# Spreading the attention normalisers by two transfers, and pairing batches so that 64-token blocks fill a matmul

## The chip, the cores and the metric

The kernel runs on one core of one Trainium2 chip. Times are device microseconds (us). Runs are compared within one call on one chip, beside runs of the kernel before; each is marked fast or slow by its clock and time, and only fast runs are compared.

## The reference

```python
scores = (q @ k.T) / sqrt(64) + cum[:, None] - cum[None, :]   # 8 batches, 8 heads, 576 tokens, causal
attn   = exp(scores - max);  attn /= attn.sum(-1)
x      = attn @ v                                             # heads side by side: 8 x 576 x 512
xk, xr = mu_k * x + (1 - mu_k) * x_prev, mu_r * x + (1 - mu_r) * x_prev
out    = sigmoid(xr @ w_r) * (relu(xk @ w_k) ** 2 @ w_v)
```

The first half is attention with a forget gate, the second a channel mix whose inputs blend each token with the one before.

## The kernel before

The attention works on pairs of heads and keeps its output transposed, 128 partitions (two heads of 64) by 576 tokens. So dividing by the softmax sum needs, on all 64 partitions of a head, the same row of 576 reciprocals. TensorE collects the sums in `den`, VectorE transposes, takes reciprocals and transposes back into `R`, and this row is spread through DRAM, for two pairs of heads (a group) at a time:

```python
PARTS = [(0, 384), (384, 192)]        # the 576 tokens in two parts ("halves")

def norm(g):
    dT = dT_ring()
    nc.vector.transpose(dT, den[:, 0:32 * QB])              # QB = 12: 384 columns
    nc.vector.reciprocal(rt[:, :, 0:2], dT[:, :, 0:2])
    nc.vector.transpose(R, rt)                              # row 32*(2*half+hh)+j is used

def spread_norm(g):
    scr = scr_ring()                                        # DRAM, [4, 32, 384]
    nc.sync.dma_start(out=scr, in_=R)
    rb = rb_ring()                                          # SBUF, [128, 2, 576]
    for half, (q0, n) in enumerate(PARTS):
        for hh in range(2):
            nc.sync.dma_start(
                out=rb[hh * D:(hh + 1) * D, :, q0:q0 + n],
                in_=scr[2 * half + hh, 0:2, 0:n].unsqueeze(0).to_broadcast([D, 2, n]))
```

Then `values` multiplies: `x = nm * rb`, once per half. The first two of sixteen groups take another way (`spread_now`, a matmul), so there are 14 such spreads. The channel mix goes in blocks of 128 tokens. A batch is 4.5 blocks, so every odd batch begins with a block that straddles two batches; it was made of two matmuls of 64 output rows each, placed side by side in the array (line L472), where other blocks take one (L468). The order of all work is written out by hand in strings of slots (`FIRST`, `ROUND`, `DRAIN`), each letter one operation.

The softmax here doesn't subtract the row's maximum and nothing guards it: scores larger than these inputs give would overflow.

Of the kernel before, what the change touches and what calls it, by code (L numbers as in the profile page):

```python
# [9 lines left out]
F32 = mybir.dt.float32  # L10
BF16 = mybir.dt.bfloat16
AF = mybir.ActivationFunctionType
ALU = mybir.AluOpType
# [19 lines left out]
PARTS = [(0, 384), (384, 192)]  # L33
QB = PARTS[0][1] // 32
# [3 lines left out]
def kernel(  # L38
# [13 lines left out]
    nc = tc.nc  # L52
    B, H, S, D = q.shape
    Dm = H * D
    Dff = moe_w_k.shape[1]
    P = 128
    SCALE = 1.0 / (D ** 0.5)
    BH = B * H
    NC = 5
    NP = BH // 2  # L60
    n_db, n_fb = Dm // P, Dff // P
    HB = S // 2
# [24 lines left out]
    mm_ring = Ring(3, [P, 512], F32, "mm", mmp)  # L87
    scr_ring = Ring(2, [4, 32, 32 * QB], F32, "scr", drp)
    a_ring = Ring(4, [P, 2, AW], BF16, "a")
    rb_ring = Ring(3, [P, 2, S], F32, "rb")  # L90
    qb_ring = Ring(2, [P, 4, P], BF16, "qb")
    kb_ring = Ring(2, [P, 4, P], BF16, "kb")
    xk_ring = Ring(2, [P, n_db, S], BF16, "xk")
    xr_ring = Ring(3, [P, n_db, S], BF16, "xr")
    sq_ring = Ring(2, [P, n_fb, S], BF16, "relusq")
    dT_ring = Ring(2, [P, QB, 32], F32, "dT")
    diff_ring = Ring(2, [P, S], BF16, "diff")
    rel_ring = Ring(3, [P, 2, HB], BF16, "rel")
# [39 lines left out]
                                   in_=(q, k, v)[i][b, hs, 4 * P:, :].rearrange("h p d -> p h d"))  # L138

    chain = [rb_ring() for _ in range(2)]  # L140
    lf, cum, wrow, zrow = (chain[i // 2][:BH, i % 2, :] for i in range(4))
    nc.scalar.dma_start(out=lf, in_=f_bh[:, :])
    load(q, qf[0], 0)
    load(k, kf[0], 0)
# [7 lines left out]
    mu_k_sb = cp.tile([P, n_db], F32)  # L152
    nc.sync.dma_start(out=mu_k_sb, in_=moe_mu_k.rearrange("(db p) -> p db", p=P))
    mu_r_sb = cp.tile([P, n_db], F32)
# [19 lines left out]
    R = cp.tile([P, QB, 32], F32)  # L174
# [5 lines left out]
    for j in range(2):  # L180
        for half in range(2):
            for hh in range(2):
                v_ = sel[:, j, half, hh * D:(hh + 1) * D]
                nc.gpsimd.affine_select(
                    out=v_, in_=v_, compare_op=ALU.not_equal, fill=1.0,
# [123 lines left out]
    def load_weights(i):  # L309
        dst, src = ((wk_sb, moe_w_k), (wr_sb, moe_w_r), (wv_sb, moe_w_v))[i]  # L310
        nc.gpsimd.dma_start(out=dst, in_=src.rearrange("(n p) d -> p n d", p=P))
# [3 lines left out]
    rbs = {}  # L315
# [31 lines left out]
    for kb in range(NC):  # L347
        for part, (p0, pn) in enumerate(PARTS):
            q0 = max(kb * P, p0)
# [29 lines left out]
    def spread_norm(g):  # L379
        scr = scr_ring()  # L380
        nc.sync.dma_start(out=scr.rearrange("g r c -> (g r) c"),
                          in_=R.rearrange("p a b -> p (a b)"))
        rb = rb_ring()
        for half, (q0, n) in enumerate(PARTS):
            for hh in range(2):
                nc.sync.dma_start(  # L386
                    out=rb[hh * D:(hh + 1) * D, :, q0:q0 + n],
                    in_=scr[2 * half + hh, 0:2, 0:n].unsqueeze(0).to_broadcast([D, 2, n]))
        for i in range(2):
            rbs[2 * g + i] = rb[:, i, :]  # L390

    def spread_now(Pi, copy):

        g, j = divmod(Pi, 2)
        if j == 0:
            rb = rb_ring()
            for i in range(2):
                rbs[2 * g + i] = rb[:, i, :]
        for half, (q0, n) in enumerate(PARTS):
            rp = mm_ring()  # L400
            nc.tensor.matmul(rp[:, 0:n], lhsT=sel[:, j, half, :],
                             rhs=R.rearrange("p a b -> p (a b)")[:, 0:n], start=True, stop=True)
            copy(rbs[Pi][:, q0:q0 + n], rp[:, 0:n])

    def values(Pi, half):
        a = aw[Pi]
        nm = mm_ring()
        b, p = divmod(Pi, PRW)
        t, tl = vw[Pi % NV], vt[b % 2]
        for kb, hf, col, o, n, last in PIECES:  # L410
            if hf != half:
                continue
            for r0 in range(0, P, 32):
                hh, d0 = divmod(r0, D)
                w = t[:, kb, hh] if kb < 4 else tl[:, 2 * p + hh]
                nc.tensor.matmul(  # L416
                    nm[r0:r0 + 32, o:o + n],
                    lhsT=w[:, d0:d0 + 32],
                    rhs=a[:, hh, col:col + n],
                    start=(kb == 0), stop=last,  # L420
                    tile_position=(0, r0))
        q0, n = PARTS[half]
        nc.vector.tensor_tensor(out=xs[Pi % NX][:, 1 + q0:1 + q0 + n], in0=nm[:, 0:n],  # L423
                                in1=rbs[Pi][:, q0:q0 + n], op=ALU.mult)
        if half == 1:
            aw.pop(Pi)
            rbs.pop(Pi)

    xks = {}
    xrs = {}  # L430

    def shift(Pi):
        b, p = divmod(Pi, PRW)
        if p == 0:
            xks[b] = xk_ring()
            xrs[b] = xr_ring()
        x = xs[Pi % NX]
        diff = diff_ring()
        nc.vector.tensor_sub(diff, x[:, 1:S + 1], x[:, 0:S])
        for dst, mu in ((xks[b], mu_k_sb), (xrs[b], mu_r_sb)):  # L440
            nc.vector.scalar_tensor_tensor(out=dst[:, p, :], in0=diff, scalar=mu[:, p:p + 1],  # L441
                                           in1=x[:, 0:S], op0=ALU.mult, op1=ALU.add)


    rsq = {}
    rels = {}

    def key_unit(b, hf, fb):
        if hf == 0 and fb == 0:
            rsq[b] = sq_ring()  # L450
        kp = mm_ring()
        for db in range(n_db):
            nc.tensor.matmul(kp[:, :HB], lhsT=wk_sb[:, db, fb * P:(fb + 1) * P],  # L453
                             rhs=xks[b][:, db, hf * HB:(hf + 1) * HB],
                             start=(db == 0), stop=(db == n_db - 1))
        if fb % 2 == 0:
            rels[b, hf] = rel_ring()
        rel = rels[b, hf]
        nc.scalar.activation(rel[:, fb % 2, :], kp[:, :HB], func=AF.Relu)  # L459
        if fb % 2 == 1:  # L460
            nc.vector.tensor_mul(rsq[b][:, fb - 1:fb + 1, hf * HB:(hf + 1) * HB], rel, rel)  # L461



    def block_mms(ps, tiles, b, t0, w, n):
        for i in range(n):
            if t0 >= 0:
                nc.tensor.matmul(ps, lhsT=tiles[b][:, i, t0:t0 + P], rhs=w[:, i, :],  # L468
                                 start=(i == 0), stop=(i == n - 1))
            else:  # L470
                for lo, t in ((0, tiles[b - 1][:, i, S - 64:S]), (64, tiles[b][:, i, 0:64])):
                    nc.tensor.matmul(ps[lo:lo + 64, :], lhsT=t, rhs=w[:, i, :],  # L472
                                     start=(i == 0), stop=(i == n - 1),
                                     tile_position=(0, lo))

    gates = {}

    def gate_unit(b, t0):
        rp = mm_ring()
        block_mms(rp, xrs, b, t0, wr_sb, n_db)  # L480
        th = th_ring()
        nc.scalar.activation(th, rp, func=AF.Tanh, scale=0.5)  # L482
        gates[b, t0] = th
# [21 lines left out]
    def queue_mix(b):  # L505
        blocks = ((0, 128), (256, 384)) if b % 2 == 0 else ((-64, 64), (192, 320, 448))
        for hf in range(2):
            for fb in range(n_fb):
                keys.append((b, hf, fb))
            for t0 in blocks[hf]:  # L510
                gvs.append((b, hf, t0, gate_unit))
                gvs.append((b, hf, t0, value_unit))

    def run_keys(n):
        for _ in range(min(n, len(keys))):
            key_unit(*keys.popleft())
# [12 lines left out]
    def finish_mix(b):  # L529
# [15 lines left out]

    FAST = 4
    FIRST = (
        "S0 C f M T F M L3 L4 M S1 k",
        "M L M c W0 S0 M S1 T D",
        "M T W2 D N k L S0 b0 S1 M M",  # L550
        "M A0 S0 c M D M L W1 b1 T S1",
        "S0 H0 D N t M A1 S1 M L c M",
        "B2 H1 T S0 W3 M A2 H2 c B3 A3 S1 M M H3 D L",
        "Z Q0 S0 L D S1 W N K1 T M k P M M",
        "M K3 S0 K3 L t K2 A D H S1 c M M G W V",
        "S0 L T D c W A N S1 H M M P M",
        "G c K2 S0 K2 M T M W V S1 D V M G A H L",
        "S0 M K2 M T L K1 D S1 N P A W M c H G",
    )
    ROUND = (  # L560
        "S0 V T L R M K2 D c A G N V S1 M K2 P G H M W",
        "S0 L V K1 W M M T k K3 S1 M D V A H R",
        "S0 W G T c L M K3 G G S1 M A D N K1 G R P M H",
        "S0 V M T G W L K2 c D S1 M A R M H K2",
    )
    DRAIN = "K5 D N G P A W H G K3 R"
    WEIGHTS = (2, 3, 5)
    av_slot = {Pi: Pi + LAG for Pi in range(FAST, NP)}
    av_slot[NP - 1] -= 1
    mix_slot = {av_slot[b * PRW + PRW - 1] + 1: b for b in range(1, B)}  # L570
# [10 lines left out]
    def step(s, op, x):  # L581
# [31 lines left out]
        elif op == "P" and s <= NP:  # L613
            spread_norm(s // 2 - 1)
        elif op in "Bb":
            spread_now(x, nc.scalar.copy if op == "B" else nc.vector.tensor_copy)
        elif op == "W":
            for Pi in [x] if x is not None else [Pi for Pi in av_slot if av_slot[Pi] == s + 1]:
                weigh(Pi)
        elif op == "A":  # L620
            for Pi in avs:
                values(Pi, 0)
                values(Pi, 1)
# [28 lines left out]
    for s in range(NP + LAG):  # L652
        if s in WEIGHTS:
            load_weights(WEIGHTS.index(s))
        if s in mix_slot:
            queue_mix(mix_slot[s])
        for op in (FIRST[s] if s < len(FIRST) else ROUND[s % PRW] if s < NP else DRAIN).split():
            step(s, op[0], int(op[1:]) if op[1:] else None)
# [36 lines left out]
```

## Time and profile before

| | before |
|---|---|
| median at the time of prediction | 295.09 us (293.64 to 297.48) |
| TensorE busy, span of the profiled run (299.94 us, marked slow) | 266.5 of 298.2 us |
| mean granted clock of TensorE | 0.977 |
| VectorE idle for the spread | 12.0 us in 12 waits |

The only profile of the kernel before is of a run marked slow, some 2% above its fastest; where a difference is as small as that, this profile does not decide it.

From the page's slices (40 equal parts of the span, clock granted to TensorE and mean share of the 16 DMA engines busy, in tenths) and its list of DMA issues (transfer, count, size, median us to landing), kernel before:

```profile
PEclk9999799978999999999988999999999999999999
DMA  7999996854759494939584594949471915131112
...
rb<-scr SPq DMA_DIRECT2D x28, 192.0 KB, 3.3
...
rb<-scr SPq DMA_DIRECT2D x28, 96.0 KB, 3.3
```

The clock is nearly full throughout. Spreads of 192 and of 96 KB land alike, 3.3 us after issue.

### The profile page before, as it was taken

How to read it: one execution, taken by the hardware profiler on the slowest of the kernel's cores; microseconds unless marked ns; L12 is line 12 of the kernel's file. 1: busy time of each engine (PE TensorE's matmuls, PEld its weight loads, DVE VectorE, ACT ScalarE, POOL GpSimd, SP SyncE). 2: the span in 40 equal slices, each digit the busy share in tenths (PEclk: the TensorE clock that was granted, in tenths of full speed). 3: DMA queues.
4: the chain of work that ended last, by engine and by line, in shares of the span. 5: the costliest groups of instructions: out<-in, count | busy, mean ns of one | idle time of the engine just before them, and what ended most of it. 6: DMA issues, size and time to landing. Idle time of an engine off the chain costs nothing.

```text
span 298.2 us, 8098 instructions
## 1 busy us (share of the span) xinstructions
PE 266.5 (89%) x3194; PEld 159.0 (53%) x3221; DVE 226.1 (76%) x462; ACT 204.6 (69%) x360; POOL 88.0 (30%) x117
## 2 busy tenths in 40 slices
PE   1677878769899999999969999999989999999994
PEld 0344545335555655566535655566555656655551
DVE  6758989787978988789847977797968886874431
ACT  4878688457877878588865887688777875424530
POOL 7294227262333333223322424132322111000000
PEclk9999799978999999999988999999999999999999
DMA  7999996854759494939584594949471915131112
GB/s 211 237 258 202 242 230 190 206 142 146 208 150 262 126 300 121 282 112 270 151 240 135 150 274 119 278 114 290 115 223 65 250 35 185 65 115 70 68 41 106
DMA packets 82438, 52.06 MB, mean 175 GB/s; under 512 B 50336, under 2 KB 77216, under 8 KB 82400
## 3 DMA queue, kind: packets, MB, share of 16 engines
q1 hardware_dynamic: 80080, 48.75, 57.5%
q0 software_dynamic: 2096, 2.62, 5.1%
q8 instruction: 25, 0.41, 0.6%
q10 hardware_dynamic: 224, 0.18, 0.3%
q14 instruction: 13, 0.11, 0.1%
HBM read 41.96 MB, written 12.19 MB: 182 GB/s over the span
## 4 chain that ended last, share of the span: by engine, by line
PE 65%; DVE 11%; DMA 9%; ACT 9%; issue 2%; SPq 2%; DVEq 0%; ACTq 0%
PE mm L468 25%; PE mm L453 15%; PE mm L416 7%; PE sc L328 7%; DMA rb<-scr 6%; ACT a L334 5%; PE sc L233 4%; PE den L364 3%; PE mm L472 3%; ACT qkT L244 2%; DMA scr<-R 2%; SPq L386 2%; DVE x L423 2%; DVE a L340 2%; ACT rel L459 1%
## 5 line engine op out<-in xcount | busy, mean ns | idle before, releaser
L334 ACT ACTIVATE a<-sc 128x1024 bf16<-128x1024 f32 (+1 forms) x128 | 100.3, 842 | 17.0 <-PE sc L328 16.8
L453 PE MATMUL mm<-xk,wk_sb 128*128 128x288 bf16 x512 | 73.9, 289 | 1.5 <-DVE x L423 0.7
L468 PE MATMUL mm<-wv_sb,relusq 128*128 128x512 bf16 x246 | 61.4, 387 | 3.3 <-DVE x L423 2.7
L459 ACT ACTIVATE rel<-mm 128x288 bf16<-128x288 f32 x128 | 48.4, 417 | 16.4 <-PE mm L453 13.0
L453 PEld LDWEIGHTS <-wk_sb 128*128 128x128 bf16 x512 | 48.0, 99 | 21.0 <-issue 6.3
L220 POOL TENSOR_TENSOR vw<-vf,wbf 128x512 bf16<-128x512 f32 x32 | 34.5, 1077 | 72.8 <-DMA vf<-in_v_dram 30.1
L461 DVE TENSOR_TENSOR relusq<-rel 128x576 bf16<-128x576 bf16 x64 | 34.2, 544 | 28.0 <-ACT rel L459 27.9
L340 DVE TENSOR_TENSOR a<-a,bound 128x256 bf16<-128x256 bf16 (+2 forms) x96 | 44.7, 477 | 3.6 <-ACT a L334 3.3
L482 ACT ACTIVATE th<-mm 128x512 f32<-128x512 f32 x36 | 21.5, 598 | 34.7 <-PE mm L468 28.7
L328 PE MATMUL sc<-qkT 64*128 64x64 bf16 (+4 forms) x384 | 37.3, 291 | 8.2 <-ACT a L334 3.8
L468 PEld LDWEIGHTS <-relusq 128*128 128x128 bf16 x256 | 23.6, 99 | 32.2 <-issue 8.1
L244 ACT COPY qkT<-sc 128x1024 bf16<-128x1024 bf16 x29 | 29.4, 1014 | 14.8 <-PE sc L237 14.3
L423 DVE TENSOR_TENSOR x<-mm,rb 128x384 bf16<-128x384 f32 x64 | 27.1, 454 | 14.7 <-DMA rb<-scr 12.0
L209 POOL CAST qb<-qf 128x512 bf16<-128x512 f32 x22 | 18.1, 825 | 62.6 <-PE sc L233 37.4
L468 PE MATMUL mm<-wr_sb,xr 128*128 128x512 bf16 x111 | 32.6, 387 | 1.6 <-issue 0.3
L489 DVE SCALAR_TENSOR_TENSOR res<-th,mm 128x512 f32<-128x512 f32 x36 | 24.6, 683 | 12.4 <-PE mm L468 8.1
L328 PEld LDWEIGHTS <-qkT 64*128 64x128 bf16 x384 | 15.0, 96 | 30.3 <-issue 24.1
L416 PE MATMUL mm<-a,vw 128*32 128x192 bf16 (+3 forms) x896 | 29.5, 267 | 0.7 <-ACT rel L459 0.4
L441 DVE SCALAR_TENSOR_TENSOR xk<-diff,mu_k_sb,x 128x576 bf16<-128x576 bf16 x32 | 26.4, 826 | 1.1
L441 DVE SCALAR_TENSOR_TENSOR xr<-diff,mu_r_sb,x 128x576 bf16<-128x576 bf16 x32 | 26.0, 812 | 0.0
L416 PEld LDWEIGHTS <-vw 128*32 128x32 bf16 x896 | 20.4, 99 | 6.8 <-issue 4.4
L233 PE MATMUL sc<-ident,qb 128*128 128x128 bf16 x128 | 13.2, 230 | 8.4 <-DVE qb L209 5.3
(67 smaller groups left out, 237.0 us busy)
## 6 DMA issues: line engine op xcount, KB each, us to landing
out_dram<-res SPq DMA_DIRECT2D x36, 256.0 KB, 3.5
qf<-in_q_dram SPq DMA_DIRECT2D x32, 256.0 KB, 4.3
kf<-in_k_dram SPq DMA_DIRECT2D x32, 256.0 KB, 4.5
vf<-in_v_dram SPq DMA_DIRECT2D x64, 128.0 KB, 4.2
rb<-scr SPq DMA_DIRECT2D x28, 192.0 KB, 3.3
scr<-R SPq DMA_DIRECT2D x14, 192.0 KB, 1.9
rb<-scr SPq DMA_DIRECT2D x28, 96.0 KB, 3.3
vt_f<-in_v_dram SPq DMA_DIRECT2D x8, 128.0 KB, 5.4
```

The lines of the kernel that those rows point to most:

```text
L220: nc.gpsimd.tensor_tensor(out=vw[Pi % NV], in0=vf[Pi % NV], in1=wbf[:, :4, 2 * Pi:2 * Pi + 2].unsqueeze(3).to_broadcast([P, 4, 2, D]), op= ...
L244: copy(qkT[Pi % NQK][:, lo * S:hi * S].rearrange("p (i s) -> p i s", i=n)[:, :, 0:4 * P] .rearrange("p i (j c) -> p i j c", c=4), tp[:, 4 ...
L328: nc.tensor.matmul(sc[:, hh, w:w + n], lhsT=t[lo:lo + D, S + kb * P:S + (kb + 1) * P], rhs=t[lo:lo + D, q0:q0 + n], start=True, stop=True)
L334: nc.scalar.activation(out=a[:, :, off:off + w], in_=sc[:, :, 0:w], func=AF.Exp, scale=SCALE)
L340: nc.vector.tensor_tensor(out=v_, in0=v_, in1=bound[:, o:o + w].unsqueeze(1).unsqueeze(1).to_broadcast([P, 2, n, w]), op=ALU.min)
L416: nc.tensor.matmul(nm[r0:r0 + 32, o:o + n], lhsT=w[:, d0:d0 + 32], rhs=a[:, hh, col:col + n], start=(kb == 0), stop=last, tile_position=(0 ...
L423: nc.vector.tensor_tensor(out=xs[Pi % NX][:, 1 + q0:1 + q0 + n], in0=nm[:, 0:n], in1=rbs[Pi][:, q0:q0 + n], op=ALU.mult)
L441: nc.vector.scalar_tensor_tensor(out=dst[:, p, :], in0=diff, scalar=mu[:, p:p + 1], in1=x[:, 0:S], op0=ALU.mult, op1=ALU.add)
L453: nc.tensor.matmul(kp[:, :HB], lhsT=wk_sb[:, db, fb * P:(fb + 1) * P], rhs=xks[b][:, db, hf * HB:(hf + 1) * HB], start=(db == 0), stop=(db ...
L459: nc.scalar.activation(rel[:, fb % 2, :], kp[:, :HB], func=AF.Relu)
L461: nc.vector.tensor_mul(rsq[b][:, fb - 1:fb + 1, hf * HB:(hf + 1) * HB], rel, rel)
L468: nc.tensor.matmul(ps, lhsT=tiles[b][:, i, t0:t0 + P], rhs=w[:, i, :], start=(i == 0), stop=(i == n - 1))
```

## The change

The intent: spread a group's normalisers by two transfers instead of four, to save two issues of 0.6 us; lay two batches side by side in `xr` and the squared keys, so that the straddling block is contiguous and takes full matmuls; and retune the slots. Core of the diff:

```diff
-        for half, (q0, n) in enumerate(PARTS):
-            for hh in range(2):
-                nc.sync.dma_start(
-                    out=rb[hh * D:(hh + 1) * D, :, q0:q0 + n],
-                    in_=scr[2 * half + hh, 0:2, 0:n].unsqueeze(0).to_broadcast([D, 2, n]))
+        for half in range(2):
+            nc.sync.dma_start(
+                out=rb[:, half].rearrange("p j c -> p (j c)"),
+                in_=scr[2 * half:2 * half + 2, 0:2, :].rearrange("g j c -> g (j c)")
+                .unsqueeze(1).to_broadcast([2, D, 2 * 32 * QB]))
...
-    xr_ring = Ring(3, [P, n_db, S], BF16, "xr")
-    sq_ring = Ring(2, [P, n_fb, S], BF16, "relusq")
+    xr_ring = Ring(2, [P, n_db, 2, S], BF16, "xr")
+    sq_ring = Ring(2, [P, n_fb, 2, S], BF16, "relusq")
...
+        t0 += b % 2 * S
         for i in range(n):
-            if t0 >= 0: ...one matmul...  else: ...two of 64 rows, side by side...
+            nc.tensor.matmul(
+                ps, lhsT=tiles[b // 2][:, i].rearrange("p b s -> p (b s)")[:, t0:t0 + P],
+                rhs=w[:, i, :], start=(i == 0), stop=(i == n - 1))
...
-        "S0 V T L R M K2 D c A G N V S1 M K2 P G H M W",      (ROUND, first of four; all slots changed)
+        "S0 V L R t M K2 V D A N S1 K2 c P G H M M W",
-    WEIGHTS = (2, 3, 5)
+    WEIGHTS = (0, 3, 5)
```

## The prediction

> **What bounds the kernel now.** I read first the busy shares of the engines, then a table of stretches of the span (busy time of each engine in each), then the chain that ended last, and last the matmuls of the two forms that the change exchanges.
>
> ```profile
> PE 266.5 (89%) x3194; PEld 159.0 (53%) x3221; DVE 226.1 (76%) x462; ACT 204.6 (69%) x360; POOL 88.0 (30%) x117
> ```
>
> TensorE leads, VectorE follows at 76%. The average hides stages, so the stretches (columns: length, then busy us and instruction count of PE, weight loads, DVE, ACT, POOL, then granted clock, DMA share, GB/s):
>
> ```profile
> 0.00:10.00 10.00, 2.89 (x22) 1.78 (x23) 6.75 (x20) 5.39 (x7) 5.80 (x23) 1.00 0.81 223
> 20.00:30.00 10.00, 7.68 (x105) 4.38 (x98) 8.27 (x19) 8.46 (x12) 5.54 (x8) 1.00 1.09 212
> 50.00:60.00 10.00, 7.10 (x92) 4.05 (x91) 8.28 (x14) 5.26 (x10) 3.43 (x4) 1.00 0.73 183
> 141.00:157.00 16.00, 13.66 (x177) 7.91 (x177) 10.85 (x23) 11.94 (x22) 5.26 (x7) 0.94 0.73 204
> 157.00:174.00 17.00, 16.95 (x220) 10.06 (x219) 14.61 (x30) 12.24 (x22) 5.13 (x5) 0.96 0.58 170
> 240.00:260.00 20.00, 19.84 (x247) 11.89 (x238) 16.41 (x35) 11.33 (x23) 2.10 (x2) 1.00 0.27 92
> ```
>
> In the same table the six stretches of the first 60 us hold 41.6 us of PE work, so PE is idle for 18.4 us there (5.3 us of that is before the first cast exists). From 60 to 280 us PE is busy 210.7 of 220: idle 9.4 us. The last 19 us hold 4.7 us of idle time. So three things can shorten the kernel: less PE work, a better start (18.4 us), or fewer holes in the middle (9.4 us). One hole is worth showing, from the chain between 141 and 157 us (start, length, what):
>
> ```profile
> 144.90 0.58 DVE R L377
> ...
> 145.50 1.86 DMA scr<-R
> ...
> 148.67 0.60 SPq L386
> 149.27 0.04 issue
> 149.31 5.35 DMA rb<-scr
> ...
> 154.74 0.38 DVE x L423
> 155.12 0.04 issue
> 155.16 0.58 PE mm L468
> ```
>
> The normaliser R goes to scratch in DRAM (1.86 us), then SyncE issues four transfers that spread it over partitions, 0.6 us each, from 147.38 on (the third is shown); the fourth is issued at 149.31, and its data have landed 5.35 us later; only then VectorE can scale the second part of x, and PE waited. The waits put it in sum: VectorE sat idle 12.0 us in 12 waits for these transfers, PE only 3.0 us (3 times) at L468 and 0.7 us at L453 for the x that followed. VectorE's idle time is mostly not PE's.
>
> **What the Trainium skill says.** (1) "TensorE: Matmul & The Clock Gate", Part 3 (packing small matmuls by row and column tiling): matmuls on different column groups of the array run at the same time; it gives 2.38x for three column tiles. The trace agrees, see below, and this decides the first half of the change. (2) "DMA: Bandwidth & Descriptors", "Anatomy of one DMA": a transfer costs about 2.0 us fixed, mostly completion, plus bytes over bandwidth (fitted there for the software path). Here the 192 KB and the 96 KB spreads both land in 3.3 us (median), so latency, not size, rules them; one outlier took 5.4. (3) "Perfetto Trace Analysis", "DMA Optimizations": few large transfers use bandwidth better, but splitting can let some start sooner. Here the split costs 0.6 us of issue each.
>
> **The change part by part.**
>
> *Middle blocks.* In each odd batch one 128-row output block straddles two batches and was made of pairs of 64-column matmuls. There are 4 such blocks, each (4 gate + 8 value) steps: 96 half matmuls become 48 full ones, 48 weight loads go. It looks like half the work. But the chain shows:
>
> ```profile
> 162.81 0.98 PE mm L472 x8
> 163.79 0.54 PE sc L328 x6
> 164.33 1.85 PE mm L472 x16
> ...
> 171.76 1.83 PE mm L468 x8
> ```
>
> Sixteen half matmuls (L472) take 1.85 us, eight full ones (L468) 1.83 us: 231 against 229 ns per step, though each half lasts 379 ns by itself. The two halves already run side by side. The gate: 0.98 against 4 x 0.229 = 0.92. Per block 2.83 - 12 x 0.229 = 0.08 us, times 4: **0.3 us**.
>
> *Spread in two transfers.* Two issues leave the path: 2 x 0.65 (with the gaps) = 1.3 us before the last landing. Bytes grow: 2 x 192 + 2 x 96 = 576 KB become 2 x 384 = 768 KB, since the second part is padded from 192 to 384 columns. At 300 GB/s (best slice of the page) 192 KB more cost 0.65 us, if nothing hides it. So some 0.7 us earlier per group; rows go from 1536 and 768 bytes (512 of them) to 3072 bytes (256), which helps. Fourteen groups; about eight of them, every second one in the loop, make VectorE wait. That is some 6 us of VectorE idle time, but of it PE can get back at most the 3.7 us it waited, and the 1.9 us event had a landing of 5.35 that issue doesn't explain. I take **2.0 us**.
>
> *Pairs of batches side by side.* xr and the squared keys get two-batch tiles: same rows, same lengths, contiguous in the inner dimension, so the DVE rows (xr 812 ns, relusq 544 ns) stay as they are. The rings get looser, not tighter. 0.
>
> *The order.* The PE order in the loop is nearly the same: values before denominators in one slot. Per loop round one transpose copy moves from ACT to DVE (ACT gives up 1.01 + 0.27, DVE takes 1.2 + 0.22 us), in 5 rounds; DVE has 8 more instructions in all. A round takes some 33 us (the copy to qkT stands on the chain at 140.57, 174.13 and 206.74), so DVE rises by about 4 points from some 82% (195 of 240 us from 20 to 260). The start is really rewritten: the scores of slot 2 come before the fp32 spread matmuls (four take 1.24 us, after a wait of 0.42 for R), and the first values come after the next scores; a pair's cast goes from DVE to POOL at about 13 us; three key units are pushed out of the crowded first rounds into the end, where PE is 99% busy anyway. In the first 50 us ACT (37.0 of 50) waits for scores 25 times over the run, 16.8 us, much of it here. Of the 13.1 us of PE idle time that isn't the first load I give the new order **2.5 us**. The load of the key weights moves from 17.8 us to the first free moment of POOL (about 7 us): it relieves the crush at 18 to 28 us, where four v loads took 9.64 us to issue, but collides with the first q and k loads. I count it as zero with a risk.
>
> Sum: 295.1 - 0.3 - 2.0 - 2.5 = **290.3 us**.
>
> **Rivals.** *PE is the bound and nothing comes of it.* For it: 210.7 of 220 busy in the middle; the middle blocks give nothing. Then only small holes close: 293 to 295. *The start and the holes close together.* If the start gives 6 us and the holes 4, the time is 285; for it speaks that the author retimed all slots around the change, and that faster landings let VectorE run ahead and feed PE; against it that PE waits only 3.7 us for x. *VectorE becomes the bound.* It gets 1.4 us more a round and the casts; if it falls behind, PE waits at x and masks: 296 to 298. Against it: 12 us of its idle time shrink at once. *The early weights delay the first q and k.* One or two us, 292 to 293; for it the DMA share of 0.81 to 0.96 in the first 20 us.
>
> **Range and chances.** A slip of any of the two guessed terms by its own size gives 286 to 295; runs of before scatter by 293.6 to 297.5. Range 285 to 294.5. Two per cent faster is 289.2, just under my number: 0.40 for faster, 0.57 for within, 0.03 for slower.
>
> **What would show it.** The full matmuls that replace L472 should take about 1.83 us for 8 and PE's busy time should fall by under 1 us; a drop of 5 or more refutes the first step. The spreads should be two issues, the last landing about 3.5 to 4 us after its issue; VectorE's wait for them should fall from 12 to 4 to 7 us and PE's wait for x from 3.7 to under 2. PE's idle time in the first 60 us should fall from 18.4 to about 16. I am wrong if the landing of the bigger transfers takes 5 us or more as a rule, if VectorE's waits stay at 12, or if the gain lies mostly in the steady stretch from 60 to 280 us.

## The result, and the profile after

The changed kernel gives correct results and took **485.36 us** (479.69 to 486.73, 4 runs) against 294.92 us for the kernel before, a ratio of 1.640 (95% interval 1.623 to 1.657). Ratios here are the mean time of one kernel's fast runs over that of the other's of the same rounds, so not quite the ratio of the medians quoted, which are of all runs. The prediction was 290.3 us.

The changed kernel's page: busy shares, two of the slice rows, and the chain that ended last by line.

```profile
PE 312.4 (65%) x3173; PEld 177.0 (37%) x3173; DVE 232.6 (48%) x470; ACT 202.6 (42%) x354; POOL 83.6 (17%) x115
...
PEclk9988968768597776967679687886958859596799
DMA  8999143333514444144342434435141232102112
...
DMA rb<-scr 50%; PE mm L474 7%; PE mm L459 6%; DMA scr<-R 5%; ACT a L338 2%; DVE x L428 2%; PE mm L421 2%; PE sc L332 2%; DVE xr L447 2%; DVE R L381 2%; DVE dT L379 2%; SPq L390 1%; PE sc L237 1%; DVE res L491 1%; DVE a L344 1%
```

Half of the chain is now one kind of transfer, against 6% before. Yet the DMA row has fallen to some 3 tenths from the moment when the spreads begin: the core waits for DMA while most of its DMA engines are idle. The waits of the changed kernel (us in total, times, longest):

```profile
DVE x L428 <- DMA rb<-scr: 181.3, 28, 8.0
...
PE mm L474 <- DVE x L428: 68.9, 14, 6.8
PE mm L459 <- DVE x L428: 65.1, 13, 7.2
```

Each of the 14 groups now stops VectorE twice, and TensorE behind it. GpSimd's wait for the loads of v grew too, from 30.1 to 129.4 us, but GpSimd is not on the chain that ended last. One group of the changed kernel on the chain (start, length, what), which answers to the one from 144.90 us in the prediction:

```profile
104.94 0.59 DVE R L381
...
105.55 1.88 DMA scr<-R
...
107.48 0.50 SPq L390
...
108.08 17.20 DMA rb<-scr
...
125.37 0.37 DVE x L428
125.74 0.04 issue
125.78 3.57 PE mm L474 x8
```

The scratch write is unchanged (1.88 us) and only one earlier issue stands before the last, as intended. But the last spread lands 17.2 us after its issue. In the timeline the first part of x starts at 117.42 us and the second at 125.37: the two transfers land some 8 us apart, one behind the other.

The list of DMA issues of the changed kernel shows this row without any landing time:

```profile
rb<-scr SPq DMA_DIRECT2D x28, 384.0 KB
```

The arithmetic of the loss: TensorE's idle time went from 298.2 - 266.5 = 31.7 us to 483.2 - 312.4 = 170.8 us, 139.1 more. Its busy time rose by 45.9 us. The work is the same or a little less, but the mean granted clock fell from 0.977 to 0.798; the holes were followed by a lower clock (TensorE had nothing to do from 443 us to 448; when it worked again, from 448.5 to 450, the granted clock was 0.50). Together 185.0 us, the difference of the spans (the profiled run before was a slow one, so against fast runs the loss is some 190 us).

### The profile page after: what moved, and what is told of

Read it like the earlier page. It is cut to its first block, busy times and chain, and to the rows that moved or that the text cites. A ratio compares the mean times of both kernels' runs of the same rounds, so it can differ in the third digit from the quotient of the medians.

```text
span 483.2 us, 8025 instructions
## 1 busy us (share of the span) xinstructions
PE 312.4 (65%) x3173; PEld 177.0 (37%) x3173; DVE 232.6 (48%) x470; ACT 202.6 (42%) x354; POOL 83.6 (17%) x115
## 2 busy tenths in 40 slices
DMA packets 78015, 54.82 MB, mean 113 GB/s; under 512 B 49496, under 2 KB 69208, under 8 KB 77976
## 4 chain that ended last, share of the span: by engine, by line
DMA 56%; PE 20%; DVE 15%; ACT 3%; issue 2%; SPq 1%; DVEq 0%; ACTq 0%
DMA rb<-scr 50%; PE mm L474 7%; PE mm L459 6%; DMA scr<-R 5%; ACT a L338 2%; DVE x L428 2%; PE mm L421 2%; PE sc L332 2%; DVE xr L447 2%; DVE R L381 2%; DVE dT L379 2%; SPq L390 1%; PE sc L237 1%; DVE res L491 1%; DVE a L344 1%
## 5 line engine op out<-in xcount | busy, mean ns | idle before, releaser
L459 PE MATMUL mm<-xk,wk_sb 128*128 128x288 bf16 x512 | 88.3, 324 | 70.6 <-DVE x L428 65.1
L428 DVE TENSOR_TENSOR x<-mm,rb 128x384 bf16<-128x384 f32 x64 | 28.2, 457 | 189.6 <-DMA rb<-scr 181.3
L474 PE MATMUL mm<-wv_sb,relusq 128*128 128x512 bf16 x288 | 83.3, 442 | 48.7 <-DVE x L428 48.7
L459 PEld LDWEIGHTS <-wk_sb 128*128 128x128 bf16 x512 | 53.3, 109 | 98.9 <-issue 79.9
L224 POOL TENSOR_TENSOR vw<-vf,wbf 128x512 bf16<-128x512 f32 x32 | 34.3, 1074 | 186.9 <-DMA vf<-in_v_dram 129.4
L474 PEld LDWEIGHTS <-relusq 128*128 128x128 bf16 x288 | 30.3, 108 | 90.5 <-issue 69.4
L474 PE MATMUL mm<-wr_sb,xr 128*128 128x512 bf16 x144 | 40.4, 407 | 20.2 <-DVE x L428 20.2
L248 ACT COPY qkT<-sc 128x1024 bf16<-128x1024 bf16 x25 | 25.3, 1012 | 48.5 <-PE sc L241 48.4
L344 DVE TENSOR_TENSOR a<-a,bound 128x256 bf16<-128x256 bf16 (+2 forms) x96 | 40.7, 437 | 5.3 <-ACT a L338 4.6
L421 PE MATMUL mm<-a,vw 128*32 128x192 bf16 (+3 forms) x896 | 33.1, 292 | 5.1 <-DVE x L428 4.9
L421 PEld LDWEIGHTS <-vw 128*32 128x32 bf16 x896 | 22.6, 108 | 11.9 <-issue 9.6
L474 PEld LDWEIGHTS <-xr 128*128 128x128 bf16 x144 | 13.8, 102 | 34.7 <-issue 24.0
L213 POOL CAST qb<-qf 128x512 bf16<-128x512 f32 x21 | 13.8, 659 | 61.3 <-PE sc L237 29.6
```

What stands on the lines that cost most here:

```text
L224: nc.gpsimd.tensor_tensor(out=vw[Pi % NV], in0=vf[Pi % NV], in1=wbf[:, :4, 2 * Pi:2 * Pi + 2].unsqueeze(3).to_broadcast([P, 4, 2, D]), op= ...
L344: nc.vector.tensor_tensor(out=v_, in0=v_, in1=bound[:, o:o + w].unsqueeze(1).unsqueeze(1).to_broadcast([P, 2, n, w]), op=ALU.min)
L421: nc.tensor.matmul(nm[r0:r0 + 32, o:o + n], lhsT=w[:, d0:d0 + 32], rhs=a[:, hh, col:col + n], start=(kb == 0), stop=last, tile_position=(0 ...
L428: nc.vector.tensor_tensor(out=xs[Pi % NX][:, 1 + q0:1 + q0 + n], in0=nm[:, 0:n], in1=rbs[Pi][:, half, 0:n], op=ALU.mult)
L459: nc.tensor.matmul(kp[:, :HB], lhsT=wk_sb[:, db, fb * P:(fb + 1) * P], rhs=xks[b][:, db, hf * HB:(hf + 1) * HB], start=(db == 0), stop=(db ...
L474: nc.tensor.matmul(ps, lhsT=tiles[b // 2][:, i].rearrange("p b s -> p (b s)")[:, t0:t0 + P], rhs=w[:, i, :], start=(i == 0), stop=(i == n ...
```

## The experiments

Theory 1 was that the transfers are slow because each is carried by only 2 of the 16 DMA engines. It rests on the Trainium skill: "DMA: Bandwidth & Descriptors", section "Why a DMA increments its semaphore by 16 and not by 1", gives the number of engines as the largest number up to 16 that divides the outermost dimension (of size above 1) of both access patterns (the shapes in which a transfer walks through its source and its destination). The section "Rules for kernel authors" of the same page says that an outermost dimension under 16, for instance "a leading zero-stride broadcast" (a repeat put outermost), confines the transfer to at most that many engines. Here the destination's is 128 and the source's 2, the pair of heads. A check on numbers: 2 x 384 KB over two engines in 17.9 us (107.48 to 125.37) is 22 GB/s for each engine; the best slice of the kernel before had 300 GB/s, 19 for each of sixteen. So two engines alone could account for the time. The traces show the number of engines more directly; they are read with the dose below. Theory 2 was the new order of slots with its early weights; theory 3 the padding (768 instead of 576 KB a group) and the longer rows.

### The change taken apart: spread alone, and four transfers

`x1_spread_only` is the kernel before with only the changed layout of `rb` and the two transfers (the first hunk of the diff above). `x2_four_transfers` is the changed kernel with

```diff
-        for half in range(2):
-            ...source [2, 64 repeats, 768]...
+        for half in range(2):
+            for hh in range(2):
+                nc.sync.dma_start(
+                    out=rb[hh * D:(hh + 1) * D, half].rearrange("p j c -> p (j c)"),
+                    in_=scr[2 * half + hh, 0:2, :].rearrange("j c -> (j c)")
+                    .unsqueeze(0).to_broadcast([D, 2 * 32 * QB]))
```

> The kernel before with nothing changed but the spread: the padded layout of rb and the two transfers, each over both groups of 64 partitions (outermost source dimension 2). Theory 1 (each of these transfers is carried by 2 of the 16 DMA engines, so 384 KB take some 8 us and the two queue behind each other): the whole loss is here, 470 to 490 us, last landing 16 to 18 us after issue. Theory 2 (the new order of slots, with its early weights, causes the loss): near 295 us, landings of 3 to 4 us.

> The changed kernel with the spread cut into four transfers, each over one group of 64 partitions (outermost dimension 64), same padded rows of 3072 bytes, same 768 KB per pair of head pairs. Theory 1 (too few engines): 287 to 294 us, landings of 3 to 4 us. Theory 3 (the padding and the long broadcast rows are slow by themselves): stays near 485 us.

Measured: x1 485.8 us (ratio 1.647), as slow as the whole change. x2 304.7 us (1.034, interval 1.023 to 1.045). The spread alone is the loss, and with the same bytes and rows it goes when each transfer covers one group. Theory 2 falls as the cause. Theory 3 falls as the main cause, but x2 is still 3.4% slower than before, which theory 1 did not expect (287 to 294 us).

### Two transfers cut the other way, and only one of them slow

`x3_two_by_head` makes one transfer per head, source [64 repeats, 2 halves, 768]; `x4_one_slow` keeps the changed form for the first half and takes x2's form for the second.

> The changed kernel with two transfers of 384 KB cut the other way: one per head, outermost dimension 64, both halves of the row in the middle dimension of 2. Same number of transfers, bytes and rows of 3072 bytes as in the changed kernel. Theory 1: 286 to 293 us, last landing 3.5 to 5 us after issue, a little better than four transfers. Theory 3 (two big transfers, or their bytes, are the trouble): near 485 us.

> The changed kernel with the first half of the queries spread as there (outermost dimension 2) and the second half by two transfers over one group each (outermost dimension 64). Theory 1: only one 384 KB transfer sits on two engines, the last landing falls from 17 to some 8 to 10 us, and 14 groups times 8 us less gives 360 to 400 us. Theory 3 (bytes): stays near 485 us.

Measured: x3 323.1 us (1.097), x4 410.7 us (1.392). The direction of theory 1 holds in both, the sizes do not. In x4 the first part of x came 11.7 us after the first issue (145.39 to 157.04) and the second 12.8 us after it (158.19), where 8 to 10 had been expected for the last landing. In x3 the transfers land in 5.3 us (median), but each half of x needs both heads, so nothing can start before the last landing; in x2 the first half needs only the first two of four. VectorE waits 34.2 us for the spread in x3, 15.2 in x2, and TensorE 29.9 us for x against 9.8. That which cut is made matters beside the number of engines is the reading of this; it was not tested apart. Why x3's transfers need 5.3 us, when those of v1 below with as many bytes need 3.9, is open (each of x3's goes to 64 partitions, each of v1's to 128).

### The dose: the repeat of 64 written as 4 x 16 and 8 x 8

```diff
-                    .unsqueeze(0).to_broadcast([D, 2 * 32 * QB]))
+                    .unsqueeze(0).unsqueeze(0).to_broadcast([4, D // 4, 2 * 32 * QB]))
```

Everything else is x2's: the same four transfers, bytes, rows and destinations.

> The four padded transfers of the run of that name, each over one group of 64 partitions, with nothing changed but how the source's repeat of 64 is written: as 4 times 16, so that the outermost dimension is 4. Same bytes, rows and destinations. Theory 1 (the outermost dimension caps the number of engines): each 192 KB sits on four engines, 2 us each behind one another, last landing 8 to 10 us after the first issue and a time of 340 to 370 us. Rival (only a transfer that spans both groups is slow): 305 us, as with 64.

> The four padded transfers with the repeat of 64 written as 8 times 8. Theory 1 with the rate that the changed kernel shows (786 KB in 17.3 us on two engines: some 23 GB/s each): eight engines need 4.3 us for the four, plus what is fixed, so a last landing of 4.5 to 6 us after its issue, a time of 305 to 325 us, between the 305 of 64 and the 398 of 4. If the cap isn't proportional, it falls outside.

Measured: 397.9 us (1.347) with 4 and 351.3 us (1.190) with 8, two executions each; both are slower than expected (340 to 370 and 305 to 325). One spread of y4_outer_four on its chain, and one of z2_outer_eight, from the last issue to landing:

```profile
143.94 9.79 DMA rb<-scr
```

```profile
153.77 7.03 DMA rb<-scr
```

The number of engines can be read from the traces. These are stretches in which little else is in flight than a spread, of the changed kernel, of y4 and of z2 (columns as in the prediction; the last three are granted clock, DMA share and GB/s):

```profile
443.00:445.00 2.00, 0.00 (x0) 0.00 (x0) 0.00 (x0) 0.00 (x0) 0.00 (x0) 0.50 0.13 52
```

```profile
359.00:361.00 2.00, 0.00 (x0) 0.00 (x0) 0.00 (x0) 0.00 (x0) 0.00 (x0) 0.50 0.25 78
```

```profile
309.00:310.00 1.00, 1.00 (x7) 0.41 (x6) 0.48 (x2) 0.51 (x2) 0.00 (x0) 1.00 0.52 122
```

The share is close to 2, 4 and 8 sixteenths. The numbers of DMA packets, from each run's page, say the same: they differ by exactly one packet for each transfer and engine (28 transfers on 2 engines in the changed kernel; 56 on 4, 8 and 16 in the others).

| outermost dimension of the source | run | first issue to second part of x, one group | DMA packets | time |
|---|---|---|---|---|
| 2 | after | 107.48 to 125.37: 17.9 us | 78015 | 485.4 us |
| 4 | y4 | 142.24 to 153.85: 11.6 us | 78183 (168 more: 56 x 4 - 28 x 2) | 397.9 us |
| 8 | z2 | 151.81 to 160.92: 9.1 us | 78407 (224 more: 56 x 4) | 351.3 us |
| 64 | x2 | 150.32 to 156.16: 5.8 us | 78855 (448 more: 56 x 8) | 304.7 us |

A zero-stride repeat, written in another way, costs 93 us (y4 against x2), and the number of engines goes with it. The time doesn't fall in proportion. An estimate: 786 KB at the 52 GB/s of two engines take 15.1 us, which leaves 2.8 of the 17.9 us; with 2.8 us fixed and the rest in proportion, four and eight engines would need 10.3 and 6.6 us. The excess over that (1.3 and 2.5 us) stays unexplained.

### The two transfers as the change wanted them, with an outermost dimension of 32

If each needed row exists 16 times in the scratch, a transfer over both groups can have the source [32 rows, 4 repeats, 768]. Destinations, bytes and number of transfers stay those of the changed kernel. `z1_outer_32` let the reciprocal write the copies; `v1_two_transfers_bt` lets the second transpose read the two columns 16 times:

```diff
-        nc.vector.transpose(R.rearrange("p a b -> p (a b)"), rt.rearrange("p a b -> p (a b)"))
+        nc.vector.transpose(R.rearrange("p a b -> p (a b)"),
+                            rt[:, :, 0:2].unsqueeze(2).to_broadcast([P, QB, 16, 2]))
...
-                in_=scr[2 * half:2 * half + 2, 0:2, :].rearrange("g j c -> g (j c)")
-                .unsqueeze(1).to_broadcast([2, D, 2 * 32 * QB]))
+                in_=scr[2 * half:2 * half + 2].rearrange("g (i j) c -> (g i) (j c)", j=2)
+                .unsqueeze(1).to_broadcast([32, 4, 2 * 32 * QB]))
```

> The changed kernel with its two transfers, one per half of the queries, over both groups of 64 partitions, 384 KB each, same destinations and padded rows; only that the reciprocal writes each normaliser row 16 times, so that the source has 32 different rows, each repeated 4 times, and its outermost dimension is 32 instead of 2. VectorE pays some 0.3 us more for each of 16 reciprocals. Theory 1 (the outermost dimension caps the engines): last landing 4 to 5 us, 296 to 306 us. If a transfer over both groups is slow for another reason (its size, its spread over partitions): above 400 us.

> The changed kernel with its two transfers of 384 KB, outermost dimension 32 as in the run that widened the reciprocal, but the 16 copies of each row come for free: the second stream transpose reads the two columns repeated 16 times, the reciprocal stays at two columns (0.30 us). If the 40.8 us of the wide reciprocal were all that held that run at 336 us: 295 to 302 us, last landing 4 to 5 us, reciprocal and transpose 0.3 and 0.6 us. If two transfers at sixteen engines are slow in another way: above 315 us.

Measured: z1 336.0 us (1.134), outside its range, for a reason that its groups show (busy us, mean ns):

```profile
L380 DVE RECIPROCAL rt<-dT 128x384 f32<-128x384 f32 x16 | 40.8, 2553 | 0.5
```

The wide reciprocal takes 2.55 us instead of 0.30; I had allowed 0.3 more. Its spreads landed in 4.0 us (median). v1, without that cost: **294.8 us** (0.993, interval 0.987 to 1.000), correct. One group of v1 on the chain, and its row of the DMA list:

```profile
147.20 0.53 SPq L391
...
147.77 4.88 DMA rb<-scr
...
152.75 0.36 DVE x L429
```

```profile
rb<-scr SPq DMA_DIRECT2D x28, 384.0 KB, 3.9
```

Two transfers of 384 KB to the same 128 partitions land in 3.9 us instead of 17, and all of the loss is gone. The packets are 78407, which is 392 more than in the changed kernel: 28 transfers on 14 more engines. Theory 1 holds. v1 has the same padded bytes and the same order as x2, yet, in another call, none of x2's 3.4%; what four padded transfers add in x2 stays open.

### The rest of the change: order and middle blocks

`y1_rest_of_change` is the changed kernel with the spread of before (four transfers, unpadded); `y2_middle_only` is y1 with the old slots and weights, so the full middle blocks alone; `y3_order_only` is the kernel before with the new slots and weights alone.

> The changed kernel with the spread undone: four transfers over one group each, rows of 1536 and 768 bytes without padding, as before; middle blocks, side-by-side tiles and the new order stay. If the padding's 192 KB more per group are what kept the run with four padded transfers at 304.7 us, this is 287 to 293 us (the start and the looser order, as the prediction had it). If the new order itself is the loss, it stays near 300 to 304 us.

> The kernel before with full matmuls for the middle blocks alone (the two-batch tiles; spread by four unpadded transfers and the order of slots as before). Prediction's first step: PE gains 0.3 us in all, so within 1 us of the kernel before, ratio 0.995 to 1.005. Rival (half matmuls cost twice): 48 steps of 0.23 us less, 11 us, ratio 0.963.

> The kernel before with the new order of slots and of weight loads alone. Prediction's term: 2.5 us gained, ratio about 0.99. Rival: the order was fitted to another spread, or loads weights too early, and loses 2 to 3 per cent by itself (ratio 1.02 to 1.03).

Measured: y1 298.6 us (1.011, interval 1.006 to 1.016), above the 287 to 293 expected; y2 294.0 us (0.998, 0.990 to 1.005); y3 299.7 us (1.013, 1.006 to 1.020), between its two expectations. The new order loses 1% by itself. Set beside y1, the 1.034 of x2 leaves some 2% (roughly); since v1 carries the padding without it, the padding's bytes alone are not its cause. In y2 eight of the full matmuls take, on the chain:

```profile
118.64 1.83 PE mm L474 x8
```

Then the order in parts, on y2: `z3_start_only` takes the new slots 0 to 5 (six of the eleven strings of `FIRST`), `z4_loop_only` the new `ROUND` and `DRAIN`.

> The kernel with full middle blocks and all else as before, plus the first six slots of the new order. In the run with the new order alone PE had 1.2 us more work done by 60 us, and lost it after that. If the start is a gain by itself: ratio 0.985 to 0.995. If the new order's start costs later what it gains: 1.00 or above.

> The kernel with full middle blocks and all else as before, plus the new order of the repeated four slots and of the drain. If the loop order (one transpose copy a round moved from ACT to VectorE, values before denominators) is what costs, the ratio is 1.01 to 1.02; if the loss of the new order lies in its slots 6 to 10 and the early weights, 0.995 to 1.005.

Measured: z3 1.000 (0.994 to 1.005), z4 0.996 (0.992 to 1.001). Neither the start nor the loop costs or gains more than these intervals allow, about half a per cent. What is left of the new order is its slots 6 to 10 and the earlier loads of weights; that these lose the 1% follows by elimination only, as it was not run alone.

### Are two transfers worth anything once they have enough engines?

`v2_old_order_bt` is v1 with the old slots. `v3_old_order_copy` is v2 with the 16 copies made by a VectorE copy between reciprocal and transpose.

> The best parts together: full middle blocks, the old order of slots, the two transfers with outermost dimension 32 and the repeated read in the transpose. Two issues fewer (1.3 us) against 192 KB more per group: VectorE's wait for the spread falls from 11.9 to some 7 to 10 us, and the time is 290 to 297 us, ratio 0.985 to 1.005. A ratio below 0.98 would beat both kernels; I don't expect it.

> The same with the 16 copies made by one small VectorE copy between reciprocal and transpose instead of by the transpose's repeated read. It costs 16 copies of about 0.5 us, 8 us of VectorE's time and 0.5 us of latency per group: ratio 1.00 to 1.02. If the repeated read gives wrong values, this is the run that stands for it.

Measured: v2 293.8 us (0.978, interval 0.970 to 0.985; the ratio rests on three of its six runs, the others being marked slow), v3 301.9 us (1.014). v2 looked like a version that beats both kernels, but y2 with four transfers had been measured on another chip. So both went to one chip, y2 as `w1_four_again`, v2 as `w2_two_again`:

> The kernel with full middle blocks, old order and four unpadded transfers, beside the next run on one chip. Prediction's first step, a second time: ratio 0.995 to 1.005 to the kernel before.

> The same kernel with two padded transfers with outermost dimension 32 and the repeated read in the transpose, beside the run with four transfers. If the two transfers, once they have enough engines, are worth something, the ratio to the kernel before is 0.975 to 0.99 and below that of the run with four by at least 0.008; if the 0.978 of the earlier run was that chip's doing, both come out within 0.005 of each other.

Measured: w1 294.0 us (0.984, 0.977 to 0.991), outside its range, and w2 295.0 us (0.986, 0.974 to 0.998). No difference between them is seen, so the lead of v2 was that of the chip or the call, not of the two transfers. VectorE's wait for the spread was 11.5 us in w1 and 10.5 in w2. That the two issues saved are paid for by the 192 KB more would fit, but was not shown. Both kernels with the old order and full middle blocks are 0 to 2% faster than the kernel before. The same kernel with four transfers has 0.998 in one call and 0.984 in another because the kernel before took longer in the second (median 299.5 us against 296.2); its own median was 294.0 both times.

## Why the prediction was wrong

**What failed: the spread.** The step read "latency, not size, rules them" and "some 0.7 us earlier per group; rows go from 1536 and 768 bytes (512 of them) to 3072 bytes (256), which helps". It counted issues, bytes and rows and took for granted that the transfer uses all 16 engines as its predecessors did. The pattern of the source had changed from [64, 2, n] to [2, 64, 768], and with it the number of engines from 16 to 2. The second part of x, which waits for the last landing, went from 7.4 us after the first issue in the group that the prediction shows (147.38 to 154.74; 5.2 if its landing had been the median of 3.3) to 17.9. Runs x1, x2, the dose and v1 put the whole loss there. The prediction cited the very page of the skill that states the rule, from another section. Its list of signs did name the one that came ("I am wrong if the landing of the bigger transfers takes 5 us or more as a rule"), but no rival in it had a mechanism for this, so its chance of a slower kernel was 0.03.

**Whose wait it is.** "VectorE's idle time is mostly not PE's" was right for waits of 1 to 3 us, which the order had room for. It doesn't scale: at 8 us a wait, TensorE stood idle for 138.9 us (68.9 + 65.1, and 4.9 at L421), beside VectorE's 181.3. And "the last landing about 3.5 to 4 us after its issue" was right for two transfers with enough engines (median 3.9 in v1), but the gain from it, 2.0 us, is not seen: w1 and w2 are alike, though their intervals are too wide to exclude it. VectorE's wait for the spread fell to 9.9 us in v1 and 10.5 in w2, not to the 4 to 7 forecast.

**Padding.** "192 KB more cost 0.65 us, if nothing hides it" is a term for one group, at most 9.1 us in 14. The median landing rose by 0.4 us with it (3.7 in x2 against 3.3). x2 against y1 suggests some 6 us in all, but v1 carries the same bytes without such a loss, so the term is neither confirmed nor refuted.

**Middle blocks.** The mechanism was right. The full matmuls that replace the halves take 1.83 us for eight, as the step used, and the rival that they save half of the work (a ratio of 0.963) is excluded by both calls. The size, 0.3 us (a ratio of 0.999), lies within the interval of y2 but above that of w1, in whose call the kernel before took longer than elsewhere; it isn't confirmed. TensorE's busy time was 264.4 us in y2 against 266.5, but at another granted clock (0.987 against 0.977), so it does not settle the size either.

**The order.** "I give the new order 2.5 us" failed in sign: y3 lost 1.3%. At first sight TensorE was 1.2 us ahead at 60 us in y3 (42.7 us busy against 41.6), and that is how the run z3 came about. But y2, with the old order, was busy 43.2 us by then and z3, with the new start, 43.1: the start gained nothing. Where the order loses is not shown; busy times from 60 to 280 us (207.3 in y3 against 210.6) can't say, as the clock granted there was higher in y3 (1.00 against 0.98).

**The early weights** remain open, being part of the remainder of the order that was not run alone.

**Two small readings** of the prediction are off, with no effect on its sum: the last stretch holds 3.9 us of idle time and not 4.7, as the span ends at 298.2 us, and 195 of 240 us are 81%.

## What to carry to other kernels

Before counting a DMA's bytes and issues, read the outermost dimension of both of its access patterns: here a pair or a short repeat put outermost left 2, 4 or 8 engines of 16, and merging transfers is just the edit that puts a small dimension there. Where a core waits for a transfer while its DMA share is low, look there first; here the same transfer could be written with a larger dimension outside. And a wait that costs little at 2 us says nothing about the same wait at 8.

## What the Trainium skill lacked or had wrong

- "DMA: Bandwidth & Descriptors", "Why a DMA increments its semaphore by 16 and not by 1": its rule fits every run (outermost 2, 4, 8, 64 and 32), but it gives no time for a small outermost dimension (the page has a bandwidth per engine elsewhere). Here 768 KB in two or four transfers took 17.9, 11.6, 9.1 and 5.8 us from first issue to use, for 2, 4, 8 and 64, so not in proportion.
- "Perfetto Trace Analysis", "DMA Optimizations", advises batching small transfers (it speaks of less than 2 KB) into larger ones. It lacks the warning that a merge may change the outermost dimension (the DMA page has the rule, but not in connection with merging); here it cost 190 us. With the engines restored, two transfers and four came out alike (0.986 and 0.984).
- No page that I read says how such a transfer looks in a profile: the landing column was empty for it and for the other SyncE transfers of the same run (after, y4 and z2), the DMA share stood at 0.13, 0.25 and 0.52 for 2, 4 and 8 engines while the chain stood on DMA, and the number of packets grew by one for each transfer and engine.
- No page that I read mentions that a stream transpose can take a repeated (zero-stride) input at no cost: 578 ns with it and without it.
- No page that I read gives the time of a VectorE reciprocal by size: 0.30 us for 24 and 2.55 us for 384 fp32 elements per partition. In this kernel such work on the way from sums to x was not hidden: the copy of v3 (16 x 0.51 = 8.2 us) went with some 10 us more than v2 (means of the fast runs, 301.4 against 291.3 us, three runs each).
